# Row maxima of the softmax weights, taken off by VectorE ahead of the exponential, in a fused dynamic convolution and feed-forward layer

## The chip, the cores and the metric

The kernel runs on one core of a Trainium2 chip. The core has five instruction streams that run side by side: TensorE (PE, with its weight loads shown as PEld), VectorE (DVE), ScalarE (ACT), GpSimd (POOL) and SyncE (SP), which here only issues transfers. Each stream is strictly in order; the streams meet at semaphores. The metric is device time in microseconds of one launch; the median of the runs is quoted. A difference is a change in that time, and a profile is one execution of the same program with its instructions recorded.

## The reference

The input `x` is 8 x 4096 x 192, and `weight_gen` gives 8 heads x 7 taps of weights for every token. The layer takes a softmax over the 7 taps, convolves causally with those weights (24 channels share a head's weight), and passes the result through a two-matrix feed-forward block with 2048 hidden channels:

```
w = weight_gen - np.max(weight_gen, axis=-1, keepdims=True)
w = np.exp(w)
w = w / (np.sum(w, axis=-1, keepdims=True) + 1e-09)
...
out = np.einsum('bshk,bskhg->bshg', w, x_unf)      # 7 taps, zero padding in front
...
h = x @ w_in          # 192 -> 2048, x is the convolution's result
g = h - np.tanh(h)
return (g @ w_out).astype(np.float32)              # 2048 -> 192
```

The weights are drawn as 0.3 times a normal variable. In exact arithmetic the softmax is the same with and without the subtraction of the maximum, save for the 1e-09, which the kernel leaves out.

## The kernel before, in words

The 32,768 tokens are cut into 32 superblocks of 1,024 tokens, numbered n = 0 to 31. A superblock lies on 128 partitions with 8 tokens each, so its softmax weights are one tile `wg_t` of 128 x 448 float32 numbers (8 tokens x 8 heads x 7 taps).

The path of a superblock's weights: SP loads them (`load_wg`, L116 to L124); ACT takes the exponential of the whole tile in place (`softmax_exp`, L167 to L174) without taking off a maximum; DVE sums the 7 taps of each row (`softmax_sum`, L183, in two halves of 128x224 in the steady part), takes the reciprocal of the 64 sums (L198, L211 in the ramp) and multiplies (`scale`, L229). In nearly all superblocks the reciprocals are written to PSUM, into spare columns of a bank that holds a transposed convolution, so that the multiplication reads one operand from SBUF and one from PSUM. For superblocks 3 and 8 the reciprocals lie in SBUF and POOL does the multiplication.

The convolution's products (`products`, L261; the multiply itself is L299) are tensor-by-tensor multiplications, both operands in SBUF, nearly all on POOL: per superblock two into a tile `pa` and one long one into `pb`. POOL also issues the DMAs that add `pb` to `pa` and one half of `pa` to the other (`dma_sum`, L236). DVE helps POOL with a token of two taps (`help`, L243): it copies 16 weights per partition into a PSUM tile (L250) and multiplies from there (L251). PE adds up what is left and transposes it, by multiplications with an identity (L384), and ACT writes the result as `convT` (L410).

The feed-forward block is what the loop over f (16 tiles of 128 hidden channels) walks through. For each f, `gemm1` (L422) lets PE make `ph` (128 x 1024 in PSUM, L427), ACT write `th = tanh(ph)` (L440), and DVE write `gt = ph - th` (L441). `ph` has three buffers, shared with the transposed convolution `pc`. The second product (L495) reads the `gt` tiles of the superblock before, in portions that a table (`plan["pairs"]`) sets between the f steps; ACT writes its results out (L514).

The order of the instructions on each engine is written out by hand: the program runs under a manual schedule, and the loop over n and f emits everything in the order in which each engine is to take it. In step n of the main loop (n from 1), the exponential of superblock n+4 stands at f = 1 (n+3 up to n = 4, and for n = 4 that of superblock 8 also at f = 4), its sums at the two f steps that `plan["sums"]` names, and its reciprocal and multiplication at the end of the step. `loads(n)` issues the load of `x` for superblock n+3 and then of the weights of superblock n+5. `wg_t` has three buffers. Superblocks 0 to 2 are handled in a ramp ahead of the first `gemm1`, and superblocks 3 and 4 in the first loop over f, that of n = 0.

Of the kernel before, what the change touches and what calls it, by code (L numbers as in the profile page):

```python
# [8 lines left out]
FP32 = mybir.dt.float32  # L9
# [3 lines left out]
AX = mybir.AxisListType  # L13
# [3 lines left out]
def kernel(  # L17
# [8 lines left out]
    nc = tc.nc  # L26

    B, S, D = x.shape
    H, K = weight_gen.shape[2], weight_gen.shape[3]
    G = D // H  # L30
    F = moe_w_in.shape[1]
    P = nc.NUM_PARTITIONS
# [3 lines left out]
    J = 8  # L36
# [4 lines left out]
    NTOT = B * NSB  # L41
# [5 lines left out]
    AHEAD = 4  # L47
# [13 lines left out]
    const = ctx.enter_context(tc.tile_pool(name="const", bufs=1))  # L61
    xpool = ctx.enter_context(tc.tile_pool(name="xpool", bufs=2))
    wgpool = ctx.enter_context(tc.tile_pool(name="wgpool", bufs=3))
    papool = ctx.enter_context(tc.tile_pool(name="papool", bufs=3))
    pbpool = ctx.enter_context(tc.tile_pool(name="pbpool", bufs=1))
    wspool = ctx.enter_context(tc.tile_pool(name="wspool", bufs=4))
# [20 lines left out]
    wg_of = {}  # L87
# [20 lines left out]
    def order(inst, other, reason):  # L108
        tc.add_manual_dep(
            inst.ins,  # L110
            other.ins.name,
            mybir.DependencyInfo(mybir.DependencyClass.Sync, mybir.DependencyReason.DATA),
            reason=reason,
        )

    def load_wg(n):  # L116
        b, s = divmod(n, NSB)
        s0 = s * TOK
        wg_t = wgpool.tile([P, J, H, K], FP32, name="wg_t")
        nc.sync.dma_start(  # L120
            out=wg_t[:],
            in_=weight_gen[b, s0 : s0 + TOK].rearrange("(p j) h k -> p j h k", p=P),
        )
        wg_of[n] = wg_t  # L124

    def load_x(n, behind=None):
        b, s = divmod(n, NSB)
        s0 = s * TOK

        x_t = xpool.tile([P, HALO + J, D], FP32, name="x_t")  # L130

        def rows(p0, p1, r0=0, r1=HALO + J):
            first = x[0, 0:1]
            return nc.sync.dma_start(  # L134
                out=x_t[p0:p1, r0:r1, :],
                in_=bass.AP(
                    tensor=first.tensor,
                    offset=first.offset + (b * S + s0 + p0 * J - HALO + r0) * D,
                    ap=[[J * D, p1 - p0], [D, r1 - r0], [1, D]],
                ),  # L140
            )

        def no_halo():
            nc.sync.dma_start(  # L144
                out=x_t[0:1, 0:HALO, :],
                in_=zero[:].rearrange("o (h d) -> o h d", h=1).to_broadcast([1, HALO, D]),
            )


        if n == 0:  # L150
            rows(0, P, HALO, HALO + J)
            rows(16, P, 0, HALO)
            rows(1, 16, 0, HALO)
            no_halo()
        else:
            dma = rows(16 if s == 0 and ZERO_AT is None else 0, P)
            if behind is not None:
                order(dma, behind, "order of the loads")
            if s == 0 and ZERO_AT is None:
                rows(0, 16, HALO)  # L160
                rows(1, 16, 0, HALO)
                no_halo()
            elif s == 0:
                halo_of[n] = no_halo
        x_of[n] = x_t

    def softmax_exp(n):  # L167
        wg_t = wg_of.pop(n)
        last_exp[0] = nc.scalar.activation(  # L169
            out=wg_t[:].rearrange("p j h k -> p (j h k)"),  # L170
            in_=wg_t[:].rearrange("p j h k -> p (j h k)"),
            func=ACT.Exp,
        )
        e_of[n] = wg_t  # L174

    def softmax_tile():
        return wspool.tile([P, J, H, K], FP32, name="wsm")
# [238 lines left out]
    def conv(n, *parts):  # L416
        pcs = []
        for _ in conv_sums(n, parts, pcs):
            pass
        conv_out(n, parts, pcs)  # L420
# [104 lines left out]
    def out_pairs(m):  # L525
        for _ in range(m):
            next(pairs)
# [59 lines left out]
    V, G_, A = nc.vector, nc.gpsimd, nc.scalar  # L587
    load_wg(0)
    load_x(0)
    load_wg(1)  # L590
    softmax_exp(0)
    for c in range(NC):
        load_w_in(c, c + 1, 0, FA, last_exp[0] if c == 0 else None)
# [19 lines left out]
    SOFT_EARLY = False  # L613
    if SOFT_EARLY:
        load_wg(2)
    load_x(1, first_halo[0])
    if not SOFT_EARLY:
        load_wg(2)
# [16 lines left out]
        hooks={6: load_w_out},  # L635
    )
    conv(0, (0, 1), (2,))
    if not SOFT_EARLY:
        softmax_exp(2)
    load_x(2)  # L640
# [4 lines left out]
    def some(sums, m):  # L645
        for _ in range(m):
            next(sums, None)
# [6 lines left out]
    for f in range(NFT):  # L654
        if f in RELIEF:
            relieved = gemm1_relieved(0, f)
        else:
            gemm1(0, f)
        for lag, step in ((1, 0), (2, 1)):
            if f - lag in RELIEF:  # L660
                relieved[step]()
        if f == 1:
            softmax_exp(3)
        if f == EARLY[0][0]:
            pcs = []
            sums = conv_sums(1, ((0, 1),), pcs, obank)
        for at, groups in EARLY:
            if f == at:
                some(sums, groups * PER)
        if f == EARLY[-1][0]:  # L670
            conv_out(1, ((0, 1),), pcs)
        if f == THIRD:
            pcs = []
            for _ in conv_sums(1, ((2,),), pcs, obank):
                pass
            conv_out(1, ((2,),), pcs)

        out_pairs(dict(()).get(f, 0))
# [10 lines left out]
    def transposes(n, chunks):  # L689
        pcs = []  # L690
        for _ in conv_sums(n, (chunks,), pcs):
            pass
        conv_out(n, (chunks,), pcs)
        return pcs[0]
# [12 lines left out]
    for n in range(1, NTOT):  # L707
        more = n < NTOT - 1
        finish = []
        plan = FIRST if n == 1 else DOUBLE if n in DOUBLE_IN else APART if n in APART_IN else STEADY  # L710

        soft = [m for m in (n + 3 if n <= AHEAD else n + 4,) if m < NTOT]
        for f in range(NFT):
            ph = gemm1(n, f)
            if n == 1:
                if f == 1:
                    load_wg(5)
                if f == 5:
                    softmax_exp(4)
                steps = ((softmax_sum, 3), (softmax_recip, 3), (softmax_sum, 4))  # L720
                for at, (step, m, h) in zip(plan["sums"], [s + (h,) for s in steps for h in (0, 1)]):
                    if f == at:
                        step(m, h * JH, (h + 1) * JH)
                if f == 5:
                    wsm_of[3] = (softmax_tile(), None, e_of[3], zr_of[3])
                    rest = products(3)
            elif f == 1:
                if soft:
                    softmax_exp(soft[0])
                if n + 2 < NTOT:  # L730
                    rest = products(n + 2)
            if n == AHEAD and f == 4:
                softmax_exp(n + 4)
            if n > 1:
                for h, at in enumerate(plan["sums"]):
                    if soft and f == at:
                        softmax_sum(soft[0], h * JH, (h + 1) * JH)
            if n == AHEAD:
                for at, (step, h) in zip(EXTRA, [(s, h) for s in (softmax_sum, softmax_recip) for h in (0, 1)]):
                    if f == at:  # L740
                        step(n + 4, h * JH, (h + 1) * JH)
                if f == EXTRA[-1]:
                    wsm_of[n + 4] = (softmax_tile(), None, e_of[n + 4], zr_of[n + 4])
            for m in (n + 2, n + 3):
                if (n, f) in HELP.get(m, ()):
                    help(m, ph, J - 1 - HELP[m].index((n, f)))
            if n + 2 < NTOT and f == (9 if n == 1 else max([b for a, b in HELP.get(n + 2, ()) if a == n] + [3])):
                rest()
            if f == (9 if n == 1 else 1) and n > STORE_FIRST:
                loads(n)  # L750
            done = 0
            for chunks, at in sorted((((0, 1), plan["t2"]), ((2,), plan["t1"])), key=lambda c: c[1]):
                if more and at[0] == f:
                    out_pairs(at[1] - done)
                    done = at[1]
                    pc = transposes(n + 1, chunks)
                    if chunks == (2,):
                        finish = [softmax_norm(m, pc[:, 0]) for m in soft]
            if f >= plan["scale"]:
                for scale_one in finish:  # L760
                    scale_one()
                finish = []
            if n + 3 in halo_of and f >= ZERO_AT:

                halo_of.pop(n + 3)()
            out_pairs(plan["pairs"][f] - done)
            if f == (9 if n == 1 else 1) and n <= STORE_FIRST:
                loads(n)
# [36 lines left out]
```

## Time and profile before

| | us |
|---|---|
| median of 3 runs | 746.48 |
| lowest and highest of the runs | 745.10 and 747.17 |
| span of the profiled execution, first to last instruction | 743.4 |
| what a run has around that span, by the median | 3.1 |
| PE busy | 722.3 (97%) |
| DVE busy | 687.4 (92%) |
| POOL busy | 654.5 (88%) |
| ACT busy | 638.8 (86%) |
| DVE busy outside `gt` (L441, 601.6) | 85.8 |

The profiled execution's own run time is not given apart from its span, so the sum of 743.4 and 3.1 stands for it. Busy time counts the time in which an engine has an instruction under way; waits for semaphores, branches and the issue of DMAs are not in it. A superblock in the steady part takes 21.85 us, which is 32 times in the span less a ramp and a tail. POOL's share is an average with an idle tail: its last product ends near 673 us.

### The profile page before, as it was taken

The page shows a single profiled execution, that of the slowest core. Times are in us where ns is not written, and L with a number is a line of the kernel's source. Part 1 is how long each engine was busy: PE and PEld are TensorE (multiplying, and loading weights), DVE is VectorE, ACT ScalarE, POOL GpSimd, SP SyncE. Part 2 cuts the span into 40 slices and gives each one's busy share as a digit, 9 for nine tenths or more (in the row PEclk, how much of TensorE's full clock was granted, in tenths as well). Part 3 has the DMA queues.
Part 4 walks back from the last instruction along what each step waited for, and adds up shares of the span by engine and source line. Part 5 has one row for each costly group of instructions (what it writes and reads, how often), then busy time and mean ns, then how long its engine had stood idle before and what let it go on. Part 6 is the DMA issues. An engine that isn't in the chain of part 4 may idle for free.

```text
span 743.4 us, 30037 instructions
## 1 busy us (share of the span) xinstructions
PE 722.3 (97%) x13616; PEld 556.5 (75%) x13616; DVE 687.4 (92%) x723; ACT 638.8 (86%) x872; POOL 654.5 (88%) x163
## 2 busy tenths in 40 slices
PE   3899999999999999999999999999999999999997
PEld 2477777778777777777777777777777777877777
DVE  7999899999999999999999999999999999988893
ACT  4888888888888888989889999898998989888882
POOL 7999999999999999999999999999999999991000
PEclk9899999999999999999999999999999999999999
DMA  8925367766567668878777977877887877776112
GB/s 236 245 46 161 135 172 185 195 179 149 124 183 184 183 185 224 210 199 203 166 202 209 236 186 204 178 195 205 221 209 195 192 181 194 193 149 110 45 45 86
DMA packets 34269, 130.06 MB, mean 175 GB/s; under 512 B 4591, under 2 KB 9439, under 8 KB 30174
## 3 DMA queue, kind: packets, MB, share of 16 engines
q0 software_dynamic: 19424, 51.12, 40.4%
q1 hardware_dynamic: 14718, 77.03, 27.6%
q8 instruction: 106, 1.74, 0.9%
q14 instruction: 21, 0.17, 0.1%
HBM read 54.52 MB, written 25.17 MB: 107 GB/s over the span
## 4 chain that ended last, share of the span: by engine, by line
PE 92%; DVE 5%; ACT 1%; issue 1%; DMA 1%; SPq 0%; DVEq 0%
PE ph L427 43%; PE obank L495 43%; PE pc L384 4%; DVE gt L441 3%; PE po L538 1%; ACT th L440 1%; DVE pa L299 1%; DMA wg_t<-in_weight_gen_dram 1%; DVE zsum L183 0%; SPq L134 0%; ACT convT L402 0%; DVE obank L211 0%; DVE pa L251 0%; DVE pb L299 0%; SPq L144 0%
## 5 line engine op out<-in xcount | busy, mean ns | idle before, releaser
L441 DVE TENSOR_TENSOR gt<-ph,th 128x1024 bf16<-128x1024 f32 x512 | 601.6, 1217 | 33.4 <-ACT th L440 23.2
L440 ACT ACTIVATE th<-ph 128x1024 f32<-128x1024 f32 x512 | 512.1, 1025 | 69.2 <-PE ph L427 60.3
L427 PE MATMUL ph<-convT,w_in 64*128 64x512 bf16 x3072 | 415.1, 379 | 5.3 <-DVE gt L441 3.3
L495 PEld LDWEIGHTS <-gt 64*128 64x128 bf16 x7936 | 355.6, 94 | 80.6 <-issue 6.3
L495 PE MATMUL obank<-w_out,gt 64*128 64x192 bf16 x7936 | 408.0, 243 | 0.9 <-issue 0.8
L299 POOL TENSOR_TENSOR pa<-x_t,wsm 128x2688 bf16<-128x2688 f32 (+3 forms) x68 | 338.9, 5232 | 0.2
L299 POOL TENSOR_TENSOR pb<-x_t,wsm 128x4608 bf16<-128x4608 f32 (+2 forms) x33 | 283.8, 8601 | 0.7 <-ACT wsm L221 0.5
L427 PEld LDWEIGHTS <-w_in 64*128 64x128 bf16 x3072 | 163.0, 94 | 86.0 <-issue 18.3
L514 ACT ACTIVATE out_sb<-obank 128x192 f32<-128x192 f32 x248 | 81.3, 328 | 11.2 <-PE obank L495 10.3
L410 ACT ACTIVATE convT<-pc 128x1024 bf16<-128x1024 f32 (+1 forms) x62 | 50.1, 810 | 2.9 <-PE pc L384 2.7
L236 POOL DMA_DIRECT2D pa<-pb x28 | 36.0, 1284 | 13.7 <-POOL pb L299 9.1
L384 PEld LDWEIGHTS <-pa 64*128 64x128 bf16 x2064 | 41.5, 100 | 6.8 <-DVE pa L299 1.1
L236 POOL DMA_DIRECT2D pa<-pa x21 | 34.7, 1651 | 9.6 <-DMA pa<-pb 8.9
L384 PE MATMUL pc<-ident,pa 64*128 64x64 bf16 x1968 | 41.2, 191 | 1.8 <-POOL pa L299 0.9
L183 DVE TENSOR_REDUCE zsum<-wg_t 128x32 f32<-128x224 f32 (+1 forms) x61 | 23.6, 387 | 2.9 <-ACT wg_t L169 2.9
L169 ACT ACTIVATE wg_t<-wg_t 128x448 f32<-128x448 f32 x32 | 18.2, 570 | 6.3 <-DMA wg_t<-in_weight_gen_dram 6.2
L251 DVE TENSOR_TENSOR pa<-x_t,ph 128x384 bf16<-128x384 f32 x34 | 18.8, 554 | 2.0 <-DVE ph L250 0.3
L229 DVE TENSOR_TENSOR wsm<-wg_t,pc 128x448 f32<-128x448 f32 x27 | 16.8, 621 | 2.5
L198 DVE RECIPROCAL pc<-zsum 128x64 f32<-128x64 f32 x27 | 14.9, 550 | 0.0
L384 PE MATMUL pc<-ident,pb 64*128 64x64 bf16 x216 | 4.9, 206 | 9.0 <-POOL pb L299 9.0
L384 PEld LDWEIGHTS <-pb 64*128 64x128 bf16 x288 | 6.3, 106 | 9.5 <-POOL pb L299 9.0
L538 PE MATMUL po<-w_out,gt 64*128 64x192 bf16 x256 | 11.2, 243 | 0.0
(27 smaller groups left out, 56.8 us busy)
## 6 DMA issues: line engine op xcount, KB each, us to landing
x_t<-in_x_dram SPq DMA_DIRECT2D x31, 1344.0 KB, 7.9
pa<-pb POOLq DMA_DIRECT2D x28, 1152.0 KB, 9.5
out_dram<-out_sb SPq DMA_DIRECT2D x31, 768.0 KB, 3.9
pa<-pa POOLq DMA_DIRECT2D x21, 768.0 KB, 7.2
wg_t<-in_weight_gen_dram SPq DMA_DIRECT2D x32, 224.0 KB, 7.1
x_t<-in_x_dram SPq DMA_DIRECT2D x1, 768.0 KB
w_out<-in_moe_w_out_dram POOLq DMA_DIRECT2D x1, 768.0 KB, 9.5
out_dram<-out_sb SPq DMA_DIRECT2D x4, 192.0 KB, 3.0
```

The source lines that it names most:

```text
L183: nc.vector.reduce_sum(out=zsum_of[n][:, j0 * H : j1 * H], in_=e_of[n][:, j0:j1].rearrange("p j h k -> p (j h) k"), axis=AX.X,)
L236: return nc.gpsimd.dma_start(out=out.rearrange("p k j d -> p k (j d)"), in_=in_.rearrange("p k j d -> p k (j d)"), accum_op=mybir.AluOpTyp ...
L251: nc.vector.tensor_mul(pa[:, 0:KH, j, :].rearrange("p k (h g) -> p k h g", h=H), bass.AP(tensor=x_v.tensor, offset=x_v.offset + j * D, ap= ...
L299: return eng.tensor_mul(prod(k0, k1)[:, :, j0:j1].rearrange("p k j (h g) -> p k (j h) g", h=H), bass.AP(tensor=x_v.tensor, offset=x_v.offs ...
L384: nc.tensor.matmul(pc[r][:, col : col + R] if home else pc[:, r, col : col + R], lhsT=prods[c][gi][r * R : (r + 1) * R, 2 * j : 2 * j + 2] ...
L410: last_conv[0] = nc.scalar.activation(out=out, in_=pc[:, :, 0:cols].rearrange("p r (cj t) -> p r cj t", t=R), func=ACT.Copy,)
L427: nc.tensor.matmul(ph[:, r, :], lhsT=w_in[r * R : (r + 1) * R, c, f * P : (f + 1) * P], rhs=convT[r * R : (r + 1) * R, c, :], start=(c == ...
L440: last_act[0] = nc.scalar.activation(out=th[:], in_=ph_f, func=ACT.Tanh)
L441: last_sub[0] = nc.vector.tensor_sub(gt[:], ph_f, th[:])
L495: mm = nc.tensor.matmul(po[:, 0:D], lhsT=g_of[n][f][r * R : (r + 1) * R, col : col + P], rhs=w_out[r * R : (r + 1) * R, f, :], start=(r == ...
L514: last_act[0] = nc.scalar.activation(out=out_sb[:, j, :], in_=po[:, 0:D], func=ACT.Copy)
L538: nc.tensor.matmul(po[:, r, 0:D], lhsT=g_of[n][f][r * R : (r + 1) * R, col : col + P], rhs=w_out[r * R : (r + 1) * R, f, :], start=(f == 0 ...
```

## The change

A new function takes the maximum over the 7 taps of every row (`reduce_max`, 128x448 to 128x64, into a new SBUF tile `rowmax` with two buffers) and subtracts it in place from the weights (`tensor_sub`, 128x448, with the 64 maxima broadcast over the taps). Both instructions are DVE's. Both inputs of the subtraction, the weights and the maxima, lie in SBUF. The exponential that follows on ACT reads what the subtraction wrote.

```diff
+    mpool = ctx.enter_context(tc.tile_pool(name="mpool", bufs=2))
...
+    def softmax_max(n):
+
+        w = wg_of[n][:].rearrange("p j h k -> p (j h) k")
+        m = mpool.tile([P, J * H], FP32, name="rowmax")
+        nc.vector.reduce_max(out=m[:], in_=w, axis=AX.X)
+        nc.vector.tensor_sub(
+            w, w, m[:].rearrange("p (n o) -> p n o", o=1).to_broadcast([P, J * H, K])
+        )
...
     load_wg(1)
+    softmax_max(0)
     softmax_exp(0)
...
+    softmax_max(1)
     load_x(1, first_halo[0])
...
     conv(0, (0, 1), (2,))
+    softmax_max(2)
     if not SOFT_EARLY:
         softmax_exp(2)
...
+        if f == 0:
+            softmax_max(3)
         if f == 1:
             softmax_exp(3)
+        if f == 14:
+            softmax_max(4)
...
             elif f == 1:
+                if soft and n < 4:
+                    softmax_max(soft[0])
                 if soft:
                     softmax_exp(soft[0])
...
             if n == AHEAD and f == 4:
+                softmax_max(n + 4)
                 softmax_exp(n + 4)
+            if n >= AHEAD and n + 5 < NTOT and f == 10:
+                softmax_max(n + 5)
```

So the pair stands, on DVE: for superblocks 0, 1 and 2 in the ramp; for 3 and 4 in the first loop, behind the `gt` of f = 0 and f = 14; for 5 and 6 at n = 2 and n = 3, behind the `gt` of f = 1 and straight ahead of the exponential; for 8 at n = 4, f = 4, again straight ahead of it; and for 9 to 31 behind the `gt` of f = 10 in step m - 5, seven steps ahead of the exponential. For superblock 7, whose exponential stands at n = 4, f = 1, no call is made, in spite of the change's name. That is 31 pairs, and DVE has 785 instructions in place of 723. The instructions of PE, ACT, POOL and SP, and their order on each engine, are the same as before.

## The prediction

> **What bounds the kernel now.** I read the shares of busy time first, then the chain that ended last:
>
> ```profile
> PE 722.3 (97%) x13616; PEld 556.5 (75%) x13616; DVE 687.4 (92%) x723; ACT 638.8 (86%) x872; POOL 654.5 (88%) x163
> PE 92%; DVE 5%; ACT 1%; issue 1%; DMA 1%; SPq 0%; DVEq 0%
> ```
>
> PE sets the end; DVE is next with 743.4 - 687.4 = 56 us idle. Whether added DVE work fits depends on where that idle time lies, so I cut four steady superblocks out, from one `gt` of f = 10 to the next (columns: window and its length, then busy time and count of PE, PEld, DVE, ACT, POOL, then clock, DMA share, GB/s), and read the waits in them:
>
> ```profile
> 436.96:458.82 21.86, 21.86 (x404) 16.83 (x402) 21.04 (x23) 19.71 (x27) 21.38 (x6) 1.00 0.82 202
> 480.92:502.77 21.85, 21.85 (x404) 16.82 (x402) 21.03 (x23) 19.71 (x27) 21.38 (x6) 1.00 0.82 202
> ...
> ACT th L440 <- PE ph L427: 6.6, 23, 0.3
> DVE gt L441 <- ACT th L440: 1.5, 4, 0.4
> ```
>
> PE is full in 21.85 us, DVE has 21.03 us of work and 0.82 us idle, of which one wait of 0.37 for a tanh. ACT waits for PE, not for DVE, so DVE keeps up, barely. The prices come from the groups by shape (busy us, mean ns of one):
>
> ```profile
> L229 DVE TENSOR_TENSOR wsm<-wg_t,pc 128x448 f32<-128x448 f32 x27 | 16.8, 621 | 2.5
> L183 DVE TENSOR_REDUCE zsum<-wg_t 128x64 f32<-128x448 f32 x3 | 1.8, 614 | 2.9 <-ACT wg_t L169 2.9
> L229 POOL TENSOR_TENSOR wsm<-wg_t,zr 128x448 f32<-128x448 f32 x2 | 2.9, 1434 | 0.0
> ```
>
> And the order in time of POOL and DVE in one steady superblock shows what each does when the pair comes (start, length, instruction):
>
> ```profile
> 451.24 1.28 POOL L236 DMA_DIRECT2D pa<-pb  x1 [0.48 <-POOL pb L299]
> 452.06 11.02 POOL L299 TENSOR_TENSOR pa<-x_t,wsm 128x2688 bf16<-128x2688 f32 x2
> 462.53 1.72 POOL L236 DMA_DIRECT2D pa<-pa  x1
> 463.30 9.32 POOL L299 TENSOR_TENSOR pb<-x_t,wsm 128x4608 bf16<-128x4608 f32 x1
> ...
> 450.14 0.56 DVE L251 TENSOR_TENSOR pa<-x_t,ph 128x384 bf16<-128x384 f32 x1
> 450.61 11.94 DVE L441 TENSOR_TENSOR gt<-ph,th 128x1024 bf16<-128x1024 f32 x10
> ```
>
> The help (L251) stands at f = 3, so the ten `gt` are f = 4 to 13, 1.194 us apart, and that of f = 10 ends at 450.61 + 7 x 1.194 = 458.97.
>
> **The change, part by part.** Nothing is removed and nothing moved on the other engines.
>
> *The maximum.* Same shape as the sum of 128x448: 0.614 us. *The subtraction, by its size.* Same shape as the `scale` row: 0.621 us. The pair is 1.235 us, 31 pairs 38.3 us.
>
> *The subtraction, by its operands.* Every two-input instruction of DVE in this trace has one input in PSUM (`ph`, `pc`, `obank`); this one has both in SBUF, as only POOL's products have. No row shows DVE with two SBUF inputs while POOL runs. Low end: it costs nothing extra, like the `scale` row at 443.16, which ran while POOL was inside a `pb` product. High end: it can't start until POOL's product under way ends. By engine it is nearest to the first, by operands to POOL's rows. What is new in it is the operands, so I take the high end, and keep the low one as a rival. Its price, superblock by superblock:
>
> - Steady (pairs of superblocks 16 to 31): DVE asks at 458.97 + 0.61 = 459.58, inside POOL's second `pa` product. To that one's end (463.08) it is 3.5; if POOL's phase is instead tied to DVE's help (the add of `pb` waits for it), POOL's DMA follows the help's end at 450.70 directly and its next DMA issue comes 0.82 + 10.47 us later, against 8.97 for DVE: 2.4. Taken: 2.95.
> - Superblocks 9 to 15: the same reading at each `gt` of f = 10 (ends 123.1, 145.6, 168.6, 191.5, 214.1, 236.8 and 259.4) plus 0.61, against the end of POOL's product at that moment: 7.9, 5.9, 4.6, 4.3, 1.5, 4.4, 1.5 = 30.1. For 9, POOL's row is a `pb` from 122.77 for 8.82.
> - Superblocks 5, 6, 8 (`gt` ends 65.4, 88.3, 115.6): 8.1, 1.6, 4.3 = 14.0. Superblocks 3 and 4: 1.6 and 2.5.
>
> The Trainium skill, page "SBUF — State Buffer", section "Who interferes with whom", speaks against this change: an instruction of VectorE with two SBUF inputs contends with a GpSimd instruction that reads SBUF, and one blocks the other for its whole length. No row here can show it; by that rule the sum is the one below with the waits, without it that of the first rival.
>
> *What queues behind.* On DVE the next `gt`, so the release of a `ph` buffer, so PE. With three buffers PE can run on for two tiles, once; DVE gives that back only from its idle time. So in a steady superblock DVE becomes the bound: 21.03 + 1.235 + 2.95 + some idle that stays. Between none and all 0.82 stays; the tanh wait of 0.37 has a cause that stays, so I take 0.3: 25.5 us, 3.67 more.
>
> *Exponential straight behind* (5, 6, 8): ACT's in-order queue holds the exponential (0.57) and with it the next tanh (1.02) until the subtraction ends; DVE then waits 1.6 more.
>
> *The wait for the load.* The maximum at f = 10 needs weights that before were needed some ten steps later. For superblock 9 SP issues the load at 120.9; loads in that stretch land in 5.8, so 126.7, 3.6 after DVE asks; for 10, 141.5 + 5.8, 1.7 late; for 11 and 12 about 0; later ones land over 10 us early. Where the subtraction then waits for POOL until 131.6 (superblock 9) or 152.1 (10), this lies inside that wait: 0. Otherwise 5.
>
> *The ramp* (0, 1, 2): DVE is the chain there, so 3 x 1.235; the exponentials of 1 and 2, done early before (8.82 and 16.90), now stand between two DVE instructions: 2 x 0.6. Together 4.9. The subtraction of 2 would ask at 18.99 + 2 x 1.235 + 0.6 + 0.61 = 22.7, with POOL's two `pb` products (15.71, pushed to 18.8; the first 5.6 long) under way: 2. Taken 7.
>
> The sum:
> - ramp 7
> - superblocks 3, 4: 2 x 1.235 + 4.1 = 6.6
> - superblocks 5, 6, 8: 14.0 + 3 x (1.235 + 1.6 - 0.8) = 20
> - superblocks 9 to 15: 30.1 + 7 x (1.235 - 0.52) = 35
> - superblocks 16 to 31: 16 x 3.67 = 59
>
> Together 127.6: a span of 871; with the 3.1 us that lie between the profiled span and the median, 874. PE's own work is unchanged, and its clock stays at 1.00, as in the window rows, or drops with more gaps; at 0.92 in the first 44 us it already does where PE waits.
>
> **The rivals.**
>
> 1. *The subtraction runs beside POOL at its row's price.* For it: DVE's rows with one SBUF input show no trace of POOL. Against: its operands. Ramp 4.9, 3 and 4 2.5, 5, 6 and 8 6.1, load waits 5, and 23 superblocks where DVE needs 21.03 + 1.235 = 22.27 in place of 21.85: at least 0.42 each, 1.235 if no idle is given back; 0.7 taken, 16. Sum 34.5: 781 (766 to 798).
> 2. *It must wait for a whole run of POOL's products, to the next DMA issue.* POOL's instructions follow each other without a gap, so DVE may never get in between. Steady superblocks are unchanged (the product that runs is the last before a DMA). For superblocks 8, 14 and 15 POOL has two more products in a row ahead: for 14, from 237.4 to 255.7, 18.3 in place of 4.4; 40 us in all: 914. Against it: POOL would have to be preferred at each of its boundaries; no row has such a request, so nothing speaks for that order either.
> 3. *Not slower: it fits into DVE's idle time.* For it: 38.3 us are added and 56 were idle. The place is the steady superblock, the price there 1.235 against 0.82 idle, and it decides from the point where the pair costs under 0.82. The rows of 0.61 and 0.62 are steady to a few ns, so this would need the pair at two thirds of its rows: 746.
>
> **How the numbers follow.** The main case has 0.80: 874, by itself 835 (every wait 2.4 and all idle given back) to 901 (3.5 in the steady ones and no idle given back). Rival 1 has 0.10, rival 2 0.08, rival 3 0.02. A tenth of the main case lies outside its own ends; 785 to 910 takes in that case, the top of rival 1 and half of rival 2: about 8 in 10. A change under 0.3% can't be told from none here. Slower has 0.97; rival 3 gives 0.02 for same and 0.01 for faster.
>
> **What the next profile would show.** A group of 31 maxima at 614 ns, which would say the first price is right. The subtraction's own row decides: busy 621 ns with idle time of about 3 us ahead of it or a length of some 3.6 us, ending when a POOL product ends, is the main case; 621 ns without idle is rival 1. DVE would take PE's place in the chain, steady superblocks would last 25 to 26 us, PE would wait for `gt`, and POOL would show idle time ahead of the add of `pb`, waiting for the help. I am wrong if POOL's phase shifts so that DVE asks in another place of POOL's round (a wait of 0 to 9 us), or if POOL gives way within a product.

## The result and the profile after

The changed kernel takes 1125.65 us (median of 4 runs, 1124.81 to 1127.46) where the kernel before takes 745.82 in the same comparison: 1.510 times as long, with a 95% interval of 1.5075 to 1.5123. The forecast was 874, its range ended at 910.

The page's busy shares and chain of the changed kernel, to be laid beside those of before:

```profile
PE 768.4 (68%) x13616; PEld 585.7 (52%) x13616; DVE 1021.3 (91%) x785; ACT 642.3 (57%) x872; POOL 655.8 (58%) x163
PE 52%; DVE 41%; ACT 4%; issue 2%; DMA 0%; DVEq 0%; ACTq 0%
```

DVE has 333.9 us more work under way, PE is busy for two thirds of the time only. The span grew by 1123.0 - 743.4 = 379.6: 333.9 of DVE's busy time and 45.7 of DVE's idle time (101.7 in place of 56.0). The two new instructions, by groups (busy us, mean ns | idle before), and the subtraction's shortest, median and longest:

```profile
L173 DVE TENSOR_TENSOR wg_t<-wg_t,rowmax 128x448 f32<-128x448 f32 x31 | 318.0, 10259 | 1.1
L172 DVE TENSOR_REDUCE rowmax<-wg_t 128x64 f32<-128x448 f32 x31 | 18.9, 609 | 2.1 <-DMA wg_t<-in_weight_gen_dram 2.1
...
L173 DVE TENSOR_TENSOR wg_t<-wg_t,rowmax x31: 624/13737/19568, 3.9 to 976.3; 128x448 f32<-128x448 f32 x31
```

The maximum costs what its row said, 609 ns. The subtraction costs 0.62 us where it runs alone and 13.7 in the median. Its waiting is recorded as its own length, not as idle time ahead of it. One steady superblock, POOL first and then DVE (start, length, instruction):

```profile
666.62 11.02 POOL L309 TENSOR_TENSOR pa<-x_t,wsm 128x2688 bf16<-128x2688 f32 x2
677.09 1.72 POOL L246 DMA_DIRECT2D pa<-pa  x1
677.87 9.32 POOL L309 TENSOR_TENSOR pb<-x_t,wsm 128x4608 bf16<-128x4608 f32 x1
703.33 1.28 POOL L246 DMA_DIRECT2D pa<-pb  x1 [16.14 <-DVE pa L261]
...
673.29 0.61 DVE L172 TENSOR_REDUCE rowmax<-wg_t 128x64 f32<-128x448 f32 x1
673.94 13.74 DVE L173 TENSOR_TENSOR wg_t<-wg_t,rowmax 128x448 f32<-128x448 f32 x1
687.60 3.47 DVE L451 TENSOR_TENSOR gt<-ph,th 128x1024 bf16<-128x1024 f32 x3
691.00 0.37 DVE L193 TENSOR_REDUCE zsum<-wg_t 128x32 f32<-128x224 f32 x1
693.45 1.23 DVE L451 TENSOR_TENSOR gt<-ph,th 128x1024 bf16<-128x1024 f32 x1 [2.08 <-ACT th L450]
```

DVE asks at 673.94, inside POOL's second `pa` product, as forecast. That product's record ends at 666.62 + 11.02 = 677.64, 3.7 us later, but the subtraction isn't let in there. It ends at 687.68, 0.49 us after POOL's long `pb` product (677.87 + 9.32 = 687.19), the last that POOL can start without DVE's help. POOL then stands still for 16.14 us, waiting for DVE's help, which stands behind the subtraction. The step of 21.85 us has become 37.5, by windows of that length (window, then busy time and count of PE, PEld, DVE, ACT, POOL, clock, DMA share, GB/s):

```profile
673.94:711.44 37.50, 23.43 (x406) 17.85 (x402) 35.12 (x24) 19.84 (x28) 21.36 (x6) 0.82 0.47 118
```

DVE fills 35.12 of 37.5; the granted clock is 0.82 where it was 1.00 before. Among the waits of the whole span (total, times, longest, us) two show who stands behind DVE:

```profile
POOL pa L246 <- DVE pa L261: 291.9, 20, 17.7
...
PE pc L394 <- DVE gt L451: 212.0, 15, 14.6
```

### The profile page after: what moved, and what is told of

The parts are those of the page before. It is cut to its first block, busy times and chain, and to the rows that moved or that the text cites. A ratio compares the mean times of both kernels' runs of the same rounds, so it can differ in the third digit from the quotient of the medians.

```text
span 1123.0 us, 30075 instructions
## 1 busy us (share of the span) xinstructions
PE 768.4 (68%) x13616; PEld 585.7 (52%) x13616; DVE 1021.3 (91%) x785; ACT 642.3 (57%) x872; POOL 655.8 (58%) x163
## 4 chain that ended last, share of the span: by engine, by line
PE 52%; DVE 41%; ACT 4%; issue 2%; DMA 0%; DVEq 0%; ACTq 0%
DVE wg_t L173 27%; PE obank L505 25%; PE ph L437 24%; DVE gt L451 12%; ACT th L450 3%; PE pc L394 3%; DVE rowmax L172 1%; PE po L548 1%; DVE pa L309 1%; DVE zsum L193 0%; DVE pb L309 0%; DMA wg_t<-in_weight_gen_dram 0%; ACT w_in L635 0%; ACT wg_t L179 0%; ACT convT L412 0%
## 5 line engine op out<-in xcount | busy, mean ns | idle before, releaser
L437 PE MATMUL ph<-convT,w_in 64*128 64x512 bf16 x3072 | 433.0, 393 | 97.3 <-DVE gt L451 92.4
L505 PE MATMUL obank<-w_out,gt 64*128 64x192 bf16 x7936 | 428.5, 251 | 29.9 <-ACT out_sb L524 29.1
L505 PEld LDWEIGHTS <-gt 64*128 64x128 bf16 x7936 | 374.3, 97 | 117.1 <-issue 45.5
L309 POOL TENSOR_TENSOR pa<-x_t,wsm 128x2688 bf16<-128x2688 f32 (+3 forms) x68 | 338.3, 5192 | 23.1 <-PE ph L437 17.3
L173 DVE TENSOR_TENSOR wg_t<-wg_t,rowmax 128x448 f32<-128x448 f32 x31 | 318.0, 10259 | 1.1
L437 PEld LDWEIGHTS <-w_in 64*128 64x128 bf16 x3072 | 167.5, 97 | 184.1 <-issue 122.4
L394 PE MATMUL pc<-ident,pa 64*128 64x64 bf16 x1968 | 47.3, 204 | 213.4 <-DVE gt L451 212.0
L394 PEld LDWEIGHTS <-pa 64*128 64x128 bf16 x2064 | 46.4, 107 | 221.3 <-issue 216.7
L172 DVE TENSOR_REDUCE rowmax<-wg_t 128x64 f32<-128x448 f32 x31 | 18.9, 609 | 2.1 <-DMA wg_t<-in_weight_gen_dram 2.1
L239 POOL TENSOR_TENSOR wsm<-wg_t,zr 128x448 f32<-128x448 f32 x2 | 2.4, 1218 | 17.5 <-ACT out_sb L524 17.5
```

Of the source, the lines that this page charges most:

```text
L172: nc.vector.reduce_max(out=m[:], in_=w, axis=AX.X)
L173: nc.vector.tensor_sub(w, w, m[:].rearrange("p (n o) -> p n o", o=1).to_broadcast([P, J * H, K]))
L309: return eng.tensor_mul(prod(k0, k1)[:, :, j0:j1].rearrange("p k j (h g) -> p k (j h) g", h=H), bass.AP(tensor=x_v.tensor, offset=x_v.offs ...
L394: nc.tensor.matmul(pc[r][:, col : col + R] if home else pc[:, r, col : col + R], lhsT=prods[c][gi][r * R : (r + 1) * R, 2 * j : 2 * j + 2] ...
L437: nc.tensor.matmul(ph[:, r, :], lhsT=w_in[r * R : (r + 1) * R, c, f * P : (f + 1) * P], rhs=convT[r * R : (r + 1) * R, c, :], start=(c == ...
L505: mm = nc.tensor.matmul(po[:, 0:D], lhsT=g_of[n][f][r * R : (r + 1) * R, col : col + P], rhs=w_out[r * R : (r + 1) * R, f, :], start=(r == ...
```

## The experiments

After the profile, theory A was: POOL's products keep out a DVE instruction that needs the same way into SBUF, and not only to the end of the product under way, but until POOL has nothing to start. The rivals: B, the length comes from the subtraction itself (in place, broadcast operand) or from its place; C, the wait has a length of its own, whatever POOL does next. The kernels below are edits of the changed kernel, the last two of the kernel with the maxima in PSUM. Step times are from the start of a `gt` of f = 0 to the next.

### The maxima in PSUM

```diff
-        m = mpool.tile([P, J * H], FP32, name="rowmax")
+        m = home      # ph[:, 0, 0 : J * H] of this f; in the ramp obank[..][:, 512 - J * H : 512]
```

> The maxima go to PSUM (spare columns of the current ph, in the ramp of obank), so the subtraction reads one input from SBUF and one from PSUM; all else is as in the changed kernel. Theory A (the subtraction's second SBUF input is what POOL's products keep waiting): the subtraction takes its 0.62 us everywhere, steps of 22.3 to 23.1 us, and a time of 766 to 798, 781 in the middle. Theory B (the length comes from the subtraction itself, in place and with a broadcast operand, or from the place of the pair): it stays at 10 us in the mean and near 1125.

Measured: 795.63, 1.0654 times before (1.0625 to 1.0682). The subtraction's row:

```profile
L172 DVE TENSOR_TENSOR wg_t<-wg_t,ph x28: 620/621/623, 28.7 to 663.2; 128x448 f32<-128x448 f32 x28
```

All 31 take 0.62 us; the steady step is 23.01. The subtraction is still in place and broadcast, at the same spot, so B falls: 330 of the 380 us hang on the second input's being in SBUF.

### The maxima alone

```diff
-        nc.vector.tensor_sub(
-            w, w, m[:].rearrange("p (n o) -> p n o", o=1).to_broadcast([P, J * H, K])
-        )
```

> The subtraction is left out, the 31 maxima stay, unused. Both theories: 31 x 0.61 us, of which 0.61 fits into the 0.82 us of idle time of a steady step and 3 x 0.61 lie in the ramp's chain: 748 to 760. Above 780 would say that the maximum itself, or the early wait for the load, is a part of the loss.

Measured: 770.18, ratio 1.0316 (1.0298 to 1.0335): 10 us over the upper end, between the two answers that the expectation gave. The steady step is 22.22 in place of 21.86, which is less than the 0.61 added. Most of the excess is early: the first `gt` starts 4.7 us later (25.43 in place of 20.77), and the steps n = 0 to 8 together last 212.4 in place of 202.0.

### One input, still from SBUF to SBUF

```diff
-        nc.vector.tensor_sub(
-            w, w, m[:].rearrange("p (n o) -> p n o", o=1).to_broadcast([P, J * H, K])
-        )
+        nc.vector.tensor_scalar(
+            out=w, in0=w, scalar1=0.5, scalar2=None, op0=mybir.AluOpType.subtract
+        )
```

> The maxima stay, and in place of the subtraction of two tensors DVE subtracts a constant in place: the same 128x448 float32, SBUF to SBUF, one input. It leaves the row's own maximum out of the result, which changes nothing in the softmax. If two SBUF inputs alone make the wait: 766 to 798, with 0.62 us or less per subtraction. If any DVE operation from SBUF to SBUF can be kept waiting by POOL: over 1000, with a mean of several us per subtraction.

Measured: 1122.0, ratio 1.5034 (1.5009 to 1.5059).

```profile
L173 DVE TENSOR_SCALAR wg_t<-wg_t x31: 393/13506/19576, 3.9 to 974.8; 128x448 f32<-128x448 f32 x31
```

One input is kept waiting just as long. Alone it takes 393 ns for 448 elements where the maximum over the same 448 takes 609, so it runs at a faster rate. The maximum also goes from SBUF to SBUF with one input and never waits. So it isn't the count of inputs, nor SBUF to SBUF as such. The Trainium skill, page "SBUF — State Buffer", section "Who interferes with whom", names both kinds that waited here: an operation with two SBUF inputs, and one in a mode that uses both ports, which a copy or an operation with a scalar can enter, while a reduction cannot; the runs agree on which operations wait. On how long, the measurement decides: the subtraction waited not only through the instruction under way, as the prediction took from that section, but through the one behind it too (13.7 us where 3.7 were left).

### POOL gives way to the subtraction

```diff
-            mul(nc.gpsimd, KA, K)
+            long = mul(nc.gpsimd, KA, K)
+            if n >= 7 and n + 2 in sub_of:
+                order(long, sub_of[n + 2], "product behind the subtraction")
```

> POOL's long product (pb, of superblock m-2) waits for the subtraction of superblock m, for m from 9 to 31; nothing else is changed. Theory A (the subtraction is let in only where POOL has no product to start): now it gets in at the end of the product under way, 2.4 to 3.5 us after it asks, plus 0.5 us; steps of n = 4 to 26 last 25 to 26.5 us in place of 37.5, and the time is 860 to 910. Rival C (the wait has a length of its own, whatever POOL does next): steps stay at 37 us or grow by what POOL loses, 1125 or more.

Measured: 951.86, ratio 1.2759 (1.274 to 1.2778). POOL and DVE in a steady superblock:

```profile
553.44 6.10 POOL L310 TENSOR_TENSOR pa<-x_t,wsm 128x3072 bf16<-128x3072 f32 x1
559.00 1.72 POOL L247 DMA_DIRECT2D pa<-pa  x1
560.12 8.97 POOL L310 TENSOR_TENSOR pb<-x_t,wsm 128x4608 bf16<-128x4608 f32 x1
...
555.84 4.20 DVE L174 TENSOR_TENSOR wg_t<-wg_t,rowmax 128x448 f32<-128x448 f32 x1
559.96 3.47 DVE L454 TENSOR_TENSOR gt<-ph,th 128x1024 bf16<-128x1024 f32 x3
563.35 0.37 DVE L194 TENSOR_REDUCE zsum<-wg_t 128x32 f32<-128x224 f32 x1
565.67 1.23 DVE L454 TENSOR_TENSOR gt<-ph,th 128x1024 bf16<-128x1024 f32 x1 [1.95 <-ACT th L453]
...
561.22 1.04 PE L397 MATMUL pc<-ident,pa 64*128 64x64 bf16 x32 [4.53 <-DVE gt L454]
562.04 1.49 PE L508 MATMUL obank<-w_out,gt 64*128 64x192 bf16 x16
563.31 1.27 PE L440 MATMUL ph<-convT,w_in 64*128 64x512 bf16 x6
```

With POOL held back the subtraction ends 0.5 us after the product under way (559.54), 4.2 in all, as theory A says; C falls. But steps last 27.8 to 29.4, not 25 to 26.5, and the time is 42 us over the upper end. The last line of DVE shows where: ahead of the `gt` of f = 14 it is idle for 1.95 us. The transposition, which PE takes behind the `gemm1` of f = 13, needs a `ph` buffer that the first `gt` behind the subtraction frees; then the transposition, a portion of the second product and the `gemm1` of f = 14 follow one another on PE, and its tanh on ACT.

### A semaphore wait of POOL for itself

```diff
-            mul(nc.gpsimd, KH, KA)
+            before_long = mul(nc.gpsimd, KH, KA)
...
-            mul(nc.gpsimd, KA, K)
+            long = mul(nc.gpsimd, KA, K)
+            if n >= 9:
+                order(long, before_long, "product behind the product")
```

> From superblock 9 on POOL's long product waits, by a semaphore, for the end of POOL's own product ahead of it; the subtraction is as in the changed kernel and nothing waits for it. In the changed kernel POOL starts an instruction some 0.5 us before the record of the one ahead ends, and there the subtraction never got in; at boundaries where POOL waited for itself it mostly did. If what is needed is a moment in which POOL has finished everything: it gets in 3.7 us after it asks, 4.2 in all, steps of 28 to 29 us, 945 to 985. If POOL's next product goes first whenever it is ready: 13.7 us and 1125.

Measured: 952.71, ratio 1.2756 (1.2735 to 1.2777).

```profile
550.59 11.01 POOL L309 TENSOR_TENSOR pa<-x_t,wsm 128x2688 bf16<-128x2688 f32 x2
561.07 1.72 POOL L246 DMA_DIRECT2D pa<-pa  x1
561.84 9.32 POOL L309 TENSOR_TENSOR pb<-x_t,wsm 128x4608 bf16<-128x4608 f32 x1
...
557.90 4.20 DVE L173 TENSOR_TENSOR wg_t<-wg_t,rowmax 128x448 f32<-128x448 f32 x1
```

POOL's records are the same as in the changed kernel: the long product starts 0.24 us after the `pa` products end, with the DMA issue between. With a wait for its own predecessor the subtraction gets in there in every steady superblock; without it, in none. So theory A needs one word more: what lets DVE in, by these two runs, is a moment in which POOL has finished everything, and POOL's records don't show one. How the two engines settle it is not shown. In a steady superblock POOL itself loses nothing by the wait.

### A gap in which POOL only writes

```diff
+    gap = const.tile([P, 1024], FP32, name="gap")
...
+            if n >= 7:
+                nc.gpsimd.memset(gap[:], 0.0)
             mul(nc.gpsimd, KA, K)
```

> From superblock 7 on POOL writes zeros to a tile of its own (128x1024 float32, an instruction that reads nothing) ahead of each long product. If what keeps the subtraction out is only that POOL's next product reads SBUF, it is let in during that write, 4.2 us after it asks: steps of 28 to 29 us as where POOL waited for it, 945 to 985. If any POOL instruction keeps it out: 13.74 us plus the length of the write, over 1125.

Measured: 1143.18, ratio 1.5339 (1.5288 to 1.5391). Two neighbouring superblocks on DVE:

```profile
689.86 14.65 DVE L174 TENSOR_TENSOR wg_t<-wg_t,rowmax 128x448 f32<-128x448 f32 x1
...
728.55 4.19 DVE L174 TENSOR_TENSOR wg_t<-wg_t,rowmax 128x448 f32<-128x448 f32 x1
```

All but one of the 16 steady subtractions (superblocks 16 to 31) wait through the write too, 13.9 to 15.1 us; one is let in after 4.19. By the records the write stands alone for some 0.9 us, then the long product starts beside it. A write between the products is no gap; why the one got in stays open (there the write starts 0.42 us after the product ahead, elsewhere about 0.2).

### A shorter last product

```diff
-            mul(nc.gpsimd, KA, K)
+            mul(nc.gpsimd, KA, K if n < 13 else KA + 1)
```

The transfer that adds it is cut alike.

> POOL's long product is cut to one tap of three from superblock 13 on (and the transfer that adds it), so taps 5 and 6 are left out of the result there; the long product then lasts about 3.1 us in place of 9.3. Theory A (the subtraction is let in where POOL runs dry, at the end of the long product): its 13.74 us become 7.5, steps from n = 10 to 26 last 31.3 us in place of 37.5, 1020 in all (1005 to 1040). Rival C (a length of its own): 13.7 us and 1125 as before.

Measured: 1035.44, ratio 1.3876 (1.3856 to 1.3897).

```profile
571.40 3.69 POOL L309 TENSOR_TENSOR pb<-x_t,wsm 128x1536 bf16<-128x1536 f32 x1
...
567.66 7.93 DVE L173 TENSOR_TENSOR wg_t<-wg_t,rowmax 128x448 f32<-128x448 f32 x1
```

The subtraction ends 0.5 us after the product's end (575.09) again: 5.6 us off the product's length (9.32 to 3.69) take 5.8 off the subtraction's (13.74 to 7.93).

### The pair at the help

```diff
-            if n >= AHEAD and n + 5 < NTOT and f == 10:
+            if n >= AHEAD and n + 5 < NTOT and f == (10 if n < 9 else 3):
```

> From n = 9 on the pair stands behind the gt of f = 3, directly ahead of DVE's help, in place of f = 10; both inputs of the subtraction are still in SBUF. POOL then has just ended its long product and waits for the help, so it has nothing to start. Theory A: the subtraction takes 0.6 to 1.5 us, steps from n = 10 on 22.5 to 24 us, and the time is 855 to 885, all that is left being lost before n = 10. Rival C: 1125 as before.

Measured: 871.54, ratio 1.17 (1.1655 to 1.1746).

```profile
627.25 9.32 POOL L309 TENSOR_TENSOR pb<-x_t,wsm 128x4608 bf16<-128x4608 f32 x1
638.30 1.28 POOL L246 DMA_DIRECT2D pa<-pb  x1 [1.72 <-DVE pa L261]
...
636.25 0.82 DVE L173 TENSOR_TENSOR wg_t<-wg_t,rowmax 128x448 f32<-128x448 f32 x1
636.99 0.17 DVE L260 COPY ph<-wsm 128x16 f32<-128x16 f32 x1
637.20 0.55 DVE L261 TENSOR_TENSOR pa<-x_t,ph 128x384 bf16<-128x384 f32 x1
```

With both inputs in SBUF the subtraction takes 0.62 to 1.3 us, because POOL ends its last product there and waits for the help. Steady steps are 23.1, as with the maxima in PSUM (23.01). Of the 125 us that are left, 99 are lost ahead of n = 9, as in the changed kernel: the first `gt` of n = 9 starts at 322.1 in both, where the kernel before is at 222.8.

### What is left with the maxima in PSUM: two placements

The first moves the pair from f = 10 to f = 5 from n = 9 on, the second takes the pairs of superblocks 5, 6 and 8 away from their exponentials.

```diff
-            if n >= AHEAD and n + 5 < NTOT and f == 10:
+            if n >= AHEAD and n + 5 < NTOT and f == (10 if n < 9 else 5):
```

> The maxima are in PSUM as in the first run, and from n = 9 on the pair stands behind the gt of f = 5 in place of f = 10. If a part of the loss is that the pair at f = 10 delays the ph buffer that the transposition ahead of f = 13 takes (DVE idles 0.55 us there for a tanh, 0.36 before), steps go from 23.01 to 22.4 or 22.7 us and the time to 783 to 791. If the place doesn't matter: 23.0 and 795.6 as in the first run.

Measured: 797.76, ratio 1.0682 (1.0663 to 1.0701), steps 23.18: a miss. The wait for a tanh, which is that of the `gt` of f = 14, does go back from 0.55 to 0.37 us, and nothing is gained.

```diff
-                if soft and n < 4:
-                    softmax_max(soft[0], ph[:, 0, 0 : J * H])
...
-                softmax_max(n + 4, ph[:, 0, 0 : J * H])
...
+            if (n, f) in ((1, 10), (2, 12), (4, 2)):
+                softmax_max({1: 5, 2: 6, 4: 8}[n], ph[:, 0, 0 : J * H])
```

> As the first run, maxima in PSUM, but the pairs of superblocks 5, 6 and 8 no longer stand straight ahead of their exponentials: behind the gt of n = 1, f = 10; n = 2, f = 12; and n = 4, f = 2. In the first run the steps n = 2, 3 and 4 were 4.1, 4.0 and 6.1 us longer than before. If that is the queue on ACT behind the exponential: steps of about 1.2 to 2 us more, and 784 to 789 in all. If it is DVE's added work alone: 795 as in the first run.

Measured: 791.97, ratio 1.0606 (1.059 to 1.0622), 3 us over the upper end of the first answer. Steps n = 2 and n = 3 fall from 26.98 and 26.70 to 24.77 and 22.45; n = 1, which took over a pair, grows from 23.39 to 24.15. Over these three steps, with the same number of pairs, that is 5.7 us less, which the place straight ahead of the exponential had cost. But n = 4 grows from 29.05 to 31.09, and there, at f = 10, the maximum of superblock 9 now waits for its weights:

```profile
139.09 0.63 DVE L171 TENSOR_REDUCE ph<-wg_t 128x64 f32<-128x448 f32 x1 [3.23 <-DMA wg_t<-in_weight_gen_dram]
```

In the first run, 11 us after the load's issue, it did not wait.

No version with the maxima beats the kernel before.

## Why the prediction was wrong

Forecast and measurement by terms, in us of the span. The waits measured are the subtractions' lengths less 0.62 each.

| term | forecast | measured |
|---|---|---|
| 31 maxima | 19.0 | 18.9 |
| 31 subtractions by size | 19.3 | 0.62 each where alone |
| wait for POOL, ramp | 2 | 2.3 |
| superblocks 3, 4 | 4.1 | 16.4 |
| superblocks 5, 6, 8 | 14.0 | 21.4 |
| superblocks 9 to 15 | 30.1 | 48.5 |
| superblocks 16 to 31 | 47.2 | 210.3 |
| all waits | 97.4 | 298.9 |
| all else, DVE's idle time above all | -8 | +43 |
| sum | 127.6 | 379.6 |

- **Failed: "it can't start until POOL's product under way ends".** This was the high end of a cost that no row showed, and it was no bound. It took for granted that POOL's end of product is a moment at which DVE gets its turn. The steady wait is not 2.95 but 13.1, because POOL's next product goes first. POOL's wait for itself shows it: the same instructions, 0.24 us apart as before, give 4.2 in place of 13.7 once POOL's next product has to wait for the end of the one ahead. This step accounts for 201 of the 252 us.
- **Rival 2 had the right kind and the wrong end.** It let POOL's run of products end at the next DMA issue, and so left the steady superblocks as they were. The DMA issue between `pa` and `pb` let the subtraction in nowhere in the steady part. It also missed superblock 5, where the trace of before has two more products behind the `pb` without a DMA issue between; the subtraction of 5 took 11.5 us, through just these. It was given 0.08 and 914.
- **Failed: "Between none and all 0.82 stays".** DVE's idle time didn't shrink, it grew by 45.7. In a steady step it is 2.38. I had counted the two tiles that PE can run ahead and stopped there; the third buffer is the transposition's at f = 13, and behind a long stop the chain through PE and ACT leaves DVE idle for 2 us. With the pair at the help this wait is 0.37 again. So even with the wait rightly bounded the sum would have been short: where the subtraction ends with the product under way, steps last 28 to 29 us and not the 25.5 of the forecast.
- **Right in kind: the operands decide, not the size.** With the maxima in PSUM the time is 795.63, within 766 to 798 of rival 1, though 15 over its middle: a steady step grows by 1.15 where 0.7 was taken, so of the pair's 1.235 hardly any fits into the idle time. But "two SBUF inputs" was too narrow; the subtraction of a constant waits as long.
- **Right: where DVE asks in the steady part, that POOL comes to be tied to the help, and the ramp.** DVE asks inside the second `pa` product, 3.7 us ahead of its end where 2.4 to 3.5 were read. The first `gt` starts 8.0 us later, 7 were forecast.
- **The load's early use: 0 as forecast, but for another reason.** DVE waits 2.1 us for weights, all in the ramp. For superblock 9 the forecast hid a load that comes 3.6 us late inside a wait for POOL; in the run that subtraction met no product of POOL (0.62 us), but DVE came to the maximum 22.7 us after the load's issue, where 2.2 were forecast, and the weights were there. In the last run it asked some 3 us after the issue, and there the lateness showed: 3.2 us.
- **Mostly wrong one by one: the waits of superblocks 3 to 15.** POOL's phase, read from the trace of before, no longer held: already at superblock 3, read as 1.6, the product under way had 5.4 us left, and with two more products behind it the subtraction took 17.0. Three of the twelve (6, 12 and 13) came within 0.2 us of their reading; with the phase moved, that is luck.
- The ends of the main case, 835 and 901, come out some 4 us further in when its own terms are added up; nothing hangs on that.
- **The other side** (rival 3) needed the pair under 0.82 in a steady step; the maximum alone, 0.61, costs 0.36 there, and the pair in PSUM 1.15.
- The clock fell (0.82 in a steady step); PE had become the waiting engine, and no run tells whether that cost anything.

## What to carry to other kernels

Before DVE is given an operation beside a GpSimd that is nearly always busy, look at where its operands lie, and at whether it runs at the faster rate, as the subtraction of a constant did (393 ns alone, where a reduction over the same numbers took 609). With one input of a two-input operation in PSUM it took 0.62 us here, with both in SBUF 13.7. A wait for another engine's instruction is not bounded by that instruction: ask what that engine starts next, and whether it ever stands still, above all when what makes it stand still is queued behind the waiter. Where such an operation can't be avoided, put it where the other engine has just run dry (0.8 us), or give that engine a semaphore wait on itself (4.2 us).

## What was not expected of the hardware

- A gap of 0.24 us in POOL's records, with a DMA issue across it, let DVE in when POOL's next product waited for the end of the one before, and not otherwise: 4.2 against 13.7 us. In the changed kernel POOL starts a `pa` product some 0.5 us before the record of the one ahead ends, so the records are not those of one unit that does one thing at a time.
- A POOL instruction that writes only (1.9 us) made the wait longer by 0.9 us and ended it early once in 16.
- An in-place subtraction of a constant waits for POOL (13.5 us in the median) while a reduction over the same numbers never does (608 to 620 ns).
- Open: for superblocks 2, 12 and 13 the subtraction was let in between two products of POOL with no wait between them that the trace shows; those starts overlapped by 0.02 to 0.04 us. For superblock 3 two boundaries that look much the same (0.05 us) let nothing in.
